# Moving ScalarE's part of weight conversions one step later, V's conversion one step sooner, and lam between the halves of q, in a kernel of linear attention and a mixer

## The chip, the cores and the metric

The kernel runs on one core of a Trainium2 chip. The metric is the device time of one execution in microseconds, the median of several. The kernel before took 690.38 us (689.95 to 690.59, 4 runs). The profile covers one execution and gives a span that is some 1.8 us shorter than the time. The granted clock is the share of its full clock that TensorE has by the profile; "half clock" means a stretch in which it is 0.5.

## The reference

Two blocks, one behind the other, shortened here to what they compute. The first is attention with a decay per head, in chunks of the sequence, the second a mixer: a low-rank product over the sequence, then two dense products with a ReLU between.

```python
# q, k, v: (4, 8, 768, 64); lam: (8,);  Dmask, lam_pow, rev_pow: powers of lam
out[chunk] = ((qb @ kb.T) * Dmask) @ vb + (qb * lam_pow) @ kv_state
kv_state   = lam_block * kv_state + (kb * rev_pow).T @ vb
x = out as (4, 768, 512)
h = x.transpose(0, 2, 1) @ U @ V          # U: 768x32, V: 32x768, float64 as w_ch1, w_ch2
u = x + h.transpose(0, 2, 1)
result = u + max(u @ w_ch1, 0) @ w_ch2    # 512 -> 2048 -> 512
```

The kernel works on 128 rows of the sequence at a time: 24 such steps, six for each of the four batches. U, V and the weights come as float64. The kernel reads them as pairs of 32-bit words and builds float32 from them by integer operations on VectorE and two ReLU passes on ScalarE that rebuild the exponent.

## The kernel before

What matters is the order of work within one step, because each engine runs its instructions in the order in which they were issued:

```python
pieces = [("prep", 0), ("scale", 0), ("scores", 0), ("inter", 0), ("masked", 0)]
for s in range(NS):
    ...
    step += [("prep", s + 1), ("scale", s + 1)] * more   # PE transposes pq, pk; ACT copies qt, kt; POOL qs, ks
    ...
    step += [("intra", s), ("state", s)]                 # PE px, pkv; ACT copy x_nat; DVE kv
    ...
    step += [("scores", s + 1)] * more                   # PE pss
    ...
    step += [("inter", s + 1), ("masked", s + 1), ("fade", s + 1)] * more   # PE px from kv; DVE sm; ACT faded
    step += [("aside", s)] * (done < 0)                  # conversion of U, V and the first weights
```

Each name stands for one product or operation of a step: pq and pk are the transposes of q and k, qt and kt their copies, pss the scores, sm the scores times the mask, px the output of the step (inter adds the part that comes from the state, intra the part from the step itself), pkv the step's addition to the state kv. qs and ks are q and k times their powers of lam, both made on GpSimd (POOL in the profile).

The conversion of one matrix is a list of pieces, each given a step in which it runs at the end, as "aside":

```python
def one():                                               # (cut)
    nc.vector.tensor_scalar(sc, hi, 20, 0x7FF, ALU.logical_shift_right, ALU.bitwise_and)
    nc.vector.tensor_scalar(m, hi, 0xFFFFF, 0x100000, ALU.bitwise_and, ALU.bitwise_or)
    nc.scalar.activation(out=sc_f, in_=sc, func=AF.Relu, bias=low_end, scale=-1.0)
    nc.scalar.activation(out=sc, in_=sc_f, func=AF.Relu, bias=high_end, scale=-float(1 << 23))
# two, three, four: one VectorE operation each; for V then
#   five:          vt = V's high bits (DVE), high(0): two ScalarE casts
#   low(1), low(3): two subtractions each on VectorE; high(2): two ScalarE casts
for steps, at in (
    (u_side, (0, 2, 2, 3, 3)),
    (v_steps(), (1, 2, 4, 4, 5, 5, 5, 6, 6, 6)),
    ...
```

Later, in step 6, `low(0)` forms pp (x times U), ScalarE copies it to pt, and `low_sum` forms pr from pt; in step 7, `mix(0)` forms pu from V and is the first to need all of V.

The start: lam is loaded behind the two halves of k on ScalarE's queue. One product (pl) spreads it over the partitions. VectorE then builds the mask (eight scans) and the powers powq (four scans) before the first masking. `keep_busy` runs products of a blank tile, four ahead of pl and one ahead of each half's transposes, so that TensorE isn't idle.

## Time and profile before

| | kernel before |
|---|---|
| time, median | 690.38 us |
| span of the profile | 688.6 us |
| TensorE busy | 674.0 us, 98% |
| TensorE idle, first 60 us | 10.3 us |
| waits of TensorE that the change aims at | lam 1.5, U's exponents 0.76, V's exponents 1.16, pt 1.91, V's low parts 2.52 us |
| stretches at half clock | one, 43.95 to 47.36 us |

TensorE is the bound, so only its idle time and its half-clock time can be won. The lines and their reading are in the prediction.

### The profile page before, as it was taken

Reading aid. Unit: us, or ns where it says so; the run is one execution under the profiler, and the core shown is the slowest. Engines: PE = TensorE matmul, PEld = TensorE weight load, DVE = VectorE, ACT = ScalarE, POOL = GpSimd, SP = SyncE. Lnnn points to the kernel's source line nnn. Section 1 sums busy time; section 2 is a strip of 40 time slices with the busy share of each in tenths; the row PEclk is TensorE's granted clock in tenths of the full one; section 3 lists DMA queues with packets and bytes.
Section 4 is the critical chain, followed back from the end, with each engine's and each line's share of the span. In section 5 each row is a group of like instructions: output and inputs, shape, how many; then the busy total and the mean of one; then the engine's idle time right before and its main releaser. Section 6 shows DMA issues by size and latency. Waiting matters only on the chain.

```text
span 688.6 us, 12580 instructions
## 1 busy us (share of the span) xinstructions
PE 674.0 (98%) x4818; PEld 546.5 (79%) x4818; DVE 498.8 (72%) x858; ACT 291.2 (42%) x543; POOL 112.2 (16%) x90
## 2 busy tenths in 40 slices
PE   7979999999999999999999999999999999999997
PEld 7858888877888888888888888888888888888885
DVE  5458888876999977777789355787586686866864
ACT  3556686645565644444456231232232322322320
POOL 3524676532000000000000000030030120300300
PEclk9999999999999999999999999999999999999999
DMA  9877887244576755556566999956354363453531
GB/s 213 198 166 187 212 212 189 69 137 171 183 273 232 272 201 198 207 205 207 205 233 241 317 299 381 327 173 186 96 184 131 92 208 99 137 169 96 165 92 61
DMA packets 131629, 131.24 MB, mean 191 GB/s; under 512 B 81330, under 2 KB 89522, under 8 KB 131570
## 3 DMA queue, kind: packets, MB, share of 16 engines
q1 hardware_dynamic: 130512, 130.18, 60.2%
q8 instruction: 38, 0.62, 0.4%
q10 hardware_dynamic: 1058, 0.26, 0.2%
q14 instruction: 21, 0.17, 0.1%
HBM read 80.09 MB, written 50.33 MB: 189 GB/s over the span
## 4 chain that ended last, share of the span: by engine, by line
PE 94%; DVE 3%; ACT 2%; issue 1%; DMA 0%; ACTq 0%; DVEq 0%
PE pz L676 26%; PE pz L809 13%; PE pz L807 13%; PE pd L686 13%; PE pd L811 13%; PE px L431 3%; PE pss L378 3%; PE put L494 2%; PE pkv L396 1%; PE px L419 1%; PE pq L338 1%; PE pk L338 1%; PE pu L477 1%; DVE sm L387 1%; PE pr L463 1%
## 5 line engine op out<-in xcount | busy, mean ns | idle before, releaser
L676 PE MATMUL pz<-u_hl,w 128*128 128x512 f32 x768 | 191.1, 398 | 0.2 <-ACT r L682 0.2
L676 PEld LDWEIGHTS pz<-u_hl,w 128*128 128x128 f32 x768 | 143.9, 188 | 36.2 <-ACT r L682 0.9
L809 PE MATMUL pz<-w_hl,m 128*128 128x512 f32 x384 | 151.6, 396 | 0.0
L807 PE MATMUL pz<-w_hl,m 128*128 128x512 f32 x384 | 151.6, 396 | 0.0
L811 PE MATMUL pd<-w_d,m 128*128 128x512 f32 x384 | 150.0, 396 | 0.0
L790 ACT ACTIVATE m<-mt 128x512 fp32r<-128x512 f32 x96 | 60.7, 632 | 195.6 <-PE pd L811 138.7
L791 DVE SCALAR_TENSOR_TENSOR m<-rm,m 128x512 fp32r<-128x512 f32 x96 | 71.5, 745 | 45.7 <-ACT m L790 45.4
L831 POOL TENSOR_TENSOR o<-o,u 128x512 f32<-128x512 f32 x20 | 29.8, 1522 | 447.5 <-DVE o L829 447.5
L691 DVE SCALAR_TENSOR_TENSOR r<-pd,r 128x512 f32<-128x512 f32 x96 | 61.8, 685 | 55.5 <-ACT r L682 41.2
L686 PE MATMUL pd<-u_d,w 128*128 128x512 f32 x384 | 98.2, 397 | 0.0
L807 PEld LDWEIGHTS pz<-w_hl,m 128*128 128x128 f32 x384 | 72.3, 188 | 17.7
L809 PEld LDWEIGHTS pz<-w_hl,m 128*128 128x128 f32 x384 | 72.3, 188 | 17.6
L811 PEld LDWEIGHTS pd<-w_d,m 128*128 128x128 f32 x384 | 72.3, 188 | 17.6
L686 PEld LDWEIGHTS pd<-u_d,w 128*128 128x128 f32 x384 | 72.2, 188 | 17.4
L682 ACT ACTIVATE r<-pz 128x512 f32<-128x512 f32 x96 | 52.0, 593 | 58.9 <-PE pz L676 58.9
L789 DVE TENSOR_SCALAR mt<-rm 128x512 uint32<-128x512 uint32 x96 | 46.2, 481 | 33.8 <-DMA rm<-r_d 33.6
L792 DVE SCALAR_TENSOR_TENSOR m<-m 128x512 fp32r<-128x512 f32 x96 | 69.0, 720 | 0.9
L192 ACT CAST w<-wt 128x512 fp32r<-128x512 f32 x32 | 19.9, 622 | 41.3 <-DVE wt L189 34.0
L387 DVE TENSOR_TENSOR sm<-pss,mask 128x512 f32<-128x512 f32 x48 | 30.7, 681 | 8.6 <-PE pss L378 8.6
L362 POOL TENSOR_TENSOR qs<-qt,powq 128x512 f32<-128x512 f32 x20 | 25.9, 1295 | 38.9 <-ACT qt L342 31.2
L431 PEld LDWEIGHTS px<-vraw,sm 128*64 128x64 f32 x768 | 25.2, 141 | 8.0 <-issue 4.1
L378 PE MATMUL pss<-qt,kt 64*128 64x128 f32 x384 | 28.6, 289 | 1.2 <-ACT kt L342 1.2
(87 smaller groups left out, 708.4 us busy)
## 6 DMA issues: line engine op xcount, KB each, us to landing
r_d<-r SPq DMA_DIRECT2D x96, 256.0 KB, 2.6
rm<-r_d SPq DMA_DIRECT2D x96, 256.0 KB, 2.7
words<-in_moe_w_ch_dram SPq DMA_DIRECT2D x30, 512.0 KB, 4.6
w_d<-w SPq DMA_DIRECT2D x16, 768.0 KB, 3.3
w_hl<-w_d SPq DMA_DIRECT2D x16, 512.0 KB, 6.5
vraw<-in_v_dram SPq DMA_DIRECT2D x24, 256.0 KB, 3.9
u_d<-x_nat SPq DMA_DIRECT2D x24, 256.0 KB, 3.3
u<-u_d SPq DMA_DIRECT2D x24, 256.0 KB, 4.2
```

What stands on the lines that cost most here:

```text
L378: nc.tensor.matmul(out=pss[:, x, a, :], lhsT=kt[half[x], a, :], rhs=qt[half[x], a, :], start=True, stop=True,)
L676: nc.tensor.matmul(out=acc[g][0], lhsT=w[:, n, ct, :], rhs=uhl[g][:, n, ct, :], start=(ct == 0 and n == 0), stop=(ct == CT - 1 and n == 1),)
L682: nc.scalar.mul(rs[g], acc[g][0], 1.0 + E)
L686: nc.tensor.matmul(out=acc[g][1], lhsT=w[:, 2, ct, :], rhs=ud[g][:, ct, :], start=(ct == 0), stop=(ct == CT - 1),)
L691: nc.vector.scalar_tensor_tensor(rs[g], acc[g][1], 4096.0, rs[g], ALU.mult, ALU.add)
L789: nc.vector.tensor_scalar(t.bitcast(U32), r.bitcast(U32), HI, None, ALU.bitwise_and)
L790: nc.scalar.activation(out=m[:, 0], in_=t, func=AF.Relu)
L791: nc.vector.scalar_tensor_tensor(m[:, 1], r, 0.0, hi, ALU.max, ALU.subtract)
L792: nc.vector.scalar_tensor_tensor(m[:, 2], hi, E, low, ALU.mult, ALU.subtract)
L807: nc.tensor.matmul(out=pz, lhsT=m[:, 0, cols], rhs=hl[:, 0], start=first, stop=False)
L809: nc.tensor.matmul(out=pz, lhsT=m[:, 1, cols], rhs=hl[:, 1], start=False, stop=end)
L811: nc.tensor.matmul(out=pd, lhsT=m[:, 2, cols], rhs=dd, start=first, stop=end)
```

## The change

The intent is to take ScalarE's conversion work out of the place where it stands between TensorE's transposes and their copies, to have V ready before the first mix (for which the last of V's low parts also moves from VectorE to GpSimd), and to start the chain from lam sooner. The diff, cut to its core:

```diff
+    late = []
+    def on_scalar(what):                      # now, or behind the next step's intra
+        if late and late[0] is None:
+            late.append(what)
+        else:
+            what()
 ...
-            nc.scalar.activation(out=sc_f, in_=sc, func=AF.Relu, bias=low_end, scale=-1.0)
-            nc.scalar.activation( ... )
+            def exponents():                  # the same two activations
+                ...
+            on_scalar(exponents)
 ...
+            if name == "q" and s == 0 and h == 0:
+                engine.dma_start(out=lam_row[:, 0:H], in_=lam.unsqueeze(0))
 ...
-        step += [("intra", s), ("state", s)]
+        step += [("intra", s), ("late", s), ("state", s)]
 ...
-            high(0)
+            on_scalar(lambda: high(0))
 ...
-            five, lambda: low(1), lambda: high(2), lambda: low(3)
+            five, lambda: low(1, nc.vector), lambda: on_scalar(lambda: high(2)),
+            lambda: low(3, nc.gpsimd),
 ...
-        (v_steps(), (1, 2, 4, 4, 5, 5, 5, 6, 6, 6)),
+        (v_steps(), (1, 1, 3, 3, 4, 4, 4, 5, 5, 5)),
 ...
+        late[:] = [None] * (s < NT)
         for step in side.pop(s, ()):
             step()
+        late[:] = late[1:]
 ...
-    nc.scalar.dma_start(out=lam_row[:, 0:H], in_=lam.unsqueeze(0))
 ...
-    keep_busy(4, "pq")
-    pl = one_bank([P, H], "pl", "pk")
+    keep_busy()                               # five blank products, none between the transposes any more
+    turn_half(0, 0, "q")                      # transposes of the first half of q, ahead of pl
+    pl = one_bank([P, H], "pl", "pt")
```

More of the change, by code (lines that the diff above doesn't have):

```diff
@@ L148, in one @@
             low_end, high_end = ends[-1][0:rows, 0:1], ends[-1][0:rows, 1:2]
-            nc.scalar.activation(out=sc_f, in_=sc, func=AF.Relu, bias=low_end, scale=-1.0)
-            nc.scalar.activation(
-                out=sc, in_=sc_f, func=AF.Relu, bias=high_end, scale=-float(1 << 23)
-            )
+            def exponents():
+                nc.scalar.activation(out=sc_f, in_=sc, func=AF.Relu, bias=low_end, scale=-1.0)
+                nc.scalar.activation(
+                    out=sc, in_=sc_f, func=AF.Relu, bias=high_end, scale=-float(1 << 23)
+                )
+            on_scalar(exponents)
         def two():
@@ L321, with keep_busy, turn_half @@
     half = [slice(0, D), slice(D, P)]
-    def keep_busy(n, tag="pss"):
-        out = (one_bank([P, C], "idle", tag) if tag == "pq" else two_banks("idle", tag)[:, 0])[:, 0:P]
-        for i in range(n):
-            nc.tensor.matmul(out=out, lhsT=blank, rhs=blank, start=True, stop=True)
-    def prep(s):
-        qt, kt = (att.tile([P, HP, P], FP32, tag=n, bufs=2, name=n) for n in ("qt", "kt"))
-        n = HP // parts(s)
-        for a0 in range(0, HP, n):
-            for name, dst, tag in (("q", qt, "pt" if a0 else "pq"), ("k", kt, "pu" if a0 else "pk")):
-                if s == 0:
-                    keep_busy(1)
-                pt = one_bank([P, n, P], "p" + name, tag)
-                for a in range(a0, a0 + n):
-                    nc.tensor.transpose(
-                        out=pt[:, a - a0, :], in_=raw[s, name][:, 2 * a : 2 * a + 2, :],
-                        identity=ident,
-                    )
-                nc.scalar.copy(dst[:, a0 : a0 + n, :], pt)
-        st[s].update(qt=qt, kt=kt)
+    def keep_busy():
+        out = one_bank([P, C], "idle", "pq")
+        for i in range(5):
+            nc.tensor.matmul(out=out[:, 0:P], lhsT=blank, rhs=blank, start=True, stop=True)
+    qts, kts = {}, {}
+    def turn_half(s, a0, name):
+        ts, tag = (qts, ("pq", "pt")) if name == "q" else (kts, ("pk", "pu"))
+        if a0 == 0:
+            ts[s] = att.tile([P, HP, P], FP32, tag=name + "t", bufs=2, name=name + "t")
+        n = HP // parts(s)
+        pt = one_bank([P, n, P], "p" + name, tag[a0 > 0])
+        for a in range(a0, a0 + n):
+            nc.tensor.transpose(
+                out=pt[:, a - a0, :], in_=raw[s, name][:, 2 * a : 2 * a + 2, :], identity=ident
+            )
+        nc.scalar.copy(ts[s][:, a0 : a0 + n, :], pt)
+    def prep(s):
+        for a0 in range(0, HP, HP // parts(s)):
+            for name in "qk":
+                if (s, a0, name) != (0, 0, "q"):
+                    turn_half(s, a0, name)
+        st[s].update(qt=qts.pop(s), kt=kts.pop(s))
         for name in "qk":
@@ L578, in high, with low @@
                 nc.scalar.copy(out, st["t"][rows])
-        def low(g):
+        def low(g, engine):
             for out, rows in parts((g,)):
-                nc.vector.tensor_tensor(
+                engine.tensor_tensor(
                     out=out, in0=st["v"][rows], in1=st["t"][rows], op=ALU.subtract
@@ L606, in aside, with on_scalar_late @@
     def aside(s):
+        late[:] = [None] * (s < NT)
         for step in side.pop(s, ()):
             step()
+        late[:] = late[1:]
+    def on_scalar_late(s):
+        for what in late:
+            what()
+        late.clear()
     ordered = ctx.enter_context(ExitStack())
@@ L630 @@
     powers()
-    run["aside"] = aside
+    run.update(aside=aside, late=on_scalar_late)
     for what, s in pieces:
```

## The prediction

> **What bounds the kernel now.** I read the page first, then the waits of TensorE, then the timeline around each of those waits, then busy time by stretches. From the page:
>
> ```profile
> PE 674.0 (98%) x4818; PEld 546.5 (79%) x4818; DVE 498.8 (72%) x858; ACT 291.2 (42%) x543; POOL 112.2 (16%) x90
> ...
> PE 94%; DVE 3%; ACT 2%; issue 1%; DMA 0%; ACTq 0%; DVEq 0%
> ```
>
> TensorE is the bound: 674.0 of 688.6 us busy, 94% of the chain that ended last. So a change that leaves its matmuls alone can win only TensorE's idle time (14.6 us), plus stretches in which it runs at half clock. The busy time by stretches (from 60 to 300 us: 239.7 of 240 us busy) puts most of the idle time into the first 60 us: 2.6 us in the first ten, then 0.9, 0.8, 1.2, 2.1 and 2.8. The waits of TensorE over the whole run name it:
>
> ```profile
> PE pu L477 <- DVE vp L582: 2.5, 1, 2.5
> PE pr L463 <- ACT pt L459: 1.9, 1, 1.9
> PE pl L626 <- DMA lam_row<-in_lam_dram: 1.5, 1, 1.5
> PE pkv L396 <- ACT kt L342: 1.2, 2, 0.8
> PE pss L378 <- ACT kt L342: 1.2, 1, 1.2
> ...
> PE px L431 <- DVE sm L387: 0.9, 2, 0.7
> ```
>
> (Who waited for whom: total us, times, longest.) Every wait the diff aims at is in this list. At the start, the timeline shows a chain:
>
> ```profile
> 1.85 0.61 ACTq L619 DMA_DIRECT2D lam_row<-in_lam_dram  x1
> ...
> 4.65 0.56 PE L626 MATMUL pl<-lam_row 1*128 1x8 f32 x2 [1.52 <-DMA lam_row<-in_lam_dram]
> ...
> 5.25 0.17 DVE L627 COPY lamb<-pl 128x8 f32<-128x8 f32 x1 [3.15 <-PE pl L626]
> 5.45 2.63 DVE L287 TENSOR_TENSOR_SCAN mask<-lamb,ident 128x128 f32<-128x128 f32 x8
> ...
> 8.37 2.22 POOL L351 TENSOR_TENSOR ks<-kraw,small 128x512 f32<-128x512 f32 x2 [7.06 <-DMA kraw<-in_k_dram]
> ...
> 8.58 2.93 DVE L300 TENSOR_TENSOR_SCAN powq<-small 128x128 f32<-128x128 f32 x4
> ...
> 11.43 1.26 DVE L387 TENSOR_TENSOR sm<-pss,mask 128x512 f32<-128x512 f32 x2
> ```
>
> lam is the third transfer on ScalarE's queue, behind both halves of k. Everything from the product with lam to the first masking is one VectorE chain without a gap; scores are ready at about 10.4 us, so VectorE sets the first px, not TensorE. The second kind of stall is ScalarE doing weight conversion between a transpose and its copy:
>
> ```profile
> 25.44 0.46 ACT L149 ACTIVATE sc<-sc,vp 128x192 f32<-128x192 uint32 x1 [0.99 <-DVE sc L145]
> ...
> 25.93 0.46 ACT L150 ACTIVATE sc<-sc,vp 128x192 uint32<-128x192 f32 x1
> ...
> 26.29 0.57 ACT L342 COPY qt<-pq 128x512 f32<-128x512 f32 x1
> 26.76 0.59 ACT L342 COPY kt<-pk 128x512 f32<-128x512 f32 x1
> ...
> 27.40 0.55 PEld L396 LDWEIGHTS pkv<-vraw,ks 128*64 128x64 f32 x16 [0.90 <-ACT kt L342]
> ```
>
> The copy qt was ready to start at about 25.2; it waits for VectorE's sc and for two exponent passes. The same happens with V's exponents at 35.09 to 36.26, and with V's high copy (the two L578 casts, 41.32 to 42.35) ahead of the copy pt, which holds pr to 42.88. Then, twice the damage of that wait:
>
> ```profile
> 40.54:43.95 3.41, 1.50 (x8) 0.50 (x6) 0.71 (x2) 2.45 (x5) 0.56 (x1) 0.99 0.82 195
> 43.95:47.36 3.41, 3.41 (x55) 3.29 (x56) 1.81 (x3) 1.29 (x3) 1.15 (x2) 0.51 0.02 3
> 47.36:50.78 3.42, 2.43 (x54) 2.01 (x52) 2.53 (x5) 3.08 (x8) 1.28 (x2) 1.00 0.51 127
> ```
>
> (Busy us of PE, PEld, DVE, ACT, POOL, then the granted clock.) After a stretch with 1.50 us of TensorE work the clock is 0.51 for 3.41 us.
>
> **What the Trainium skill says.** (1) "TensorE: Matmul & The Clock Gate", Part 1, has a clock gate that drops to half after an idle window of about 3.4 us, a free-running one, and starts in that state. The trace agrees: half clock for 3.41 us above, and the first transposes are 421 ns each against 272 later, until about 9.6 us. (2) The same page, "Architectural detail", calls ScalarE and VectorE strict FIFO. The trace agrees: qt sits behind the exponents although its transpose had ended. (3) "SBUF — State Buffer", "Who interferes with whom": a VectorE operation with two SBUF inputs, or in a two-port mode, and a GpSimd operation that reads SBUF exclude each other. The trace agrees: the powq scans take 392 to 1209 ns, the longest while ks runs, and at 54.78 us a conversion takes 1.03 us beside ks where its twin takes 0.42. (4) "DMA: Bandwidth & Descriptors", "Queues, rings and completion order": SP and ACT each own one ring on the same 16 engines, descriptors consumed in ring order. So lam behind one half of q should land sooner than behind two of k; the trace of before shows only the second: 1.85 to about 4.5 us.
>
> **The change, part by part.**
>
> *Start.* lam moves behind the first q half on SP's queue: issue at about 1.3 instead of 1.85, landing at my estimate 3.6 instead of 4.5 (q halves take a median 2.9 us to landing from 0.74). TensorE first does five blank products instead of four (8 passes took 2.08 us, so 10 take about 2.5: 1.05 to 3.55), then two transposes at 0.21 spacing, then pl, 0.56: end about 4.6 instead of 5.21. The VectorE chain moves as a block, sm and px with it: 0.6 us. The four single blank products (8 passes at 0.21 = 1.7 us) leave prep, which only gives TensorE slack ahead of sm: worth nothing on the path.
>
> *U's exponents* go behind the next step's x_nat copy. There ScalarE has about 4.29 us per step and 2.84 us of work (0.59 x 3 + 1.07), so 0.92 us fits. Removes the 0.76 us wait of pkv.
>
> *V's exponents* (2 x 0.61) likewise, in step 4: 2.84 + 1.22 = 4.06, just inside 4.29. Removes 1.16 us.
>
> *V's first high copy* (1.03 us) runs in step 5, before pp exists. Then pt can follow pp at once: the 40.97 to 42.88 gap goes, 1.91 us. With it goes the reason for the half clock. What that cost, from the same groups elsewhere on the chain: px 1.90 against 1.08, pkv 0.85 against 0.47, pss 1.40 against 1.09, pr 1.13 against 0.86: 0.82 + 0.38 + 0.31 + 0.27 = 1.78 us.
>
> *V's low parts* move a step earlier, and two of the four go to GpSimd. Now they take 49.51 to 52.74 on VectorE and hold mix until 52.30. With them in step 5 and the second high copy (1.05 us) after x_nat of step 6, mix finds all ready: pkv, pss, px and transposes (0.47 + 1.09 + 0.62 + 1.03 = 3.2 us) lie between intra and mix, the copies need 0.59 + 1.05. Removes 2.52 us.
>
> Sum of gains: 0.6 + 0.76 + 1.16 + 1.91 + 1.78 + 2.52 = 8.7 us. After 60 us TensorE is busy throughout, so what is won there should reach the end whole.
>
> *New costs, estimates.* Step 3 now carries on VectorE both U's last two operations and V's first three: 0.35 + 0.36 + 0.34 + 0.35 + 0.55 = 1.95 us, in a gap between sm and the next kv add of some 1.98 us, with GpSimd's qs (1.28) and ks falling into it. I take 0.7 us of new wait there. And at the start TensorE loses the blank products and will have done scores and the next transposes by about 8.5 us, then idle until px at about 11.5: 3 us, near the stretch that cost the clock at 40.54. Half clock for one such stretch costs 1.7 us; at a little under one chance in two, 0.8 us. 8.7 - 0.7 - 0.8 = 7.2.
>
> **Rivals.** (a) *All 8.7 us arrive*: 681.8. For it: the waits are single and named, and ScalarE and GpSimd have room. Against: VectorE's step 3 is full to the brim. (b) *The cold start and VectorE eat half*: the clock is slow from 11 to 15 us and kv waits behind V's conversion for one GpSimd operation after another: minus 1.7 and minus 2.0, so 685.5. For it: the scans beside ks took two to three times as long. Against: the freed TensorE work gives prep room, and the released clock may come earlier than 9.6 us. (c) *Transfers become the bound in the first 40 us*, where the DMA share is 0.9 to 1.0 and q, k and v alone are 768 KB per 4.29 us: gains vanish until 40 us, leaving 6.2 - 0.7: 685. Against: q for step 7 is issued at 25.95 and used at 39.88, nine microseconds after landing, and no TensorE wait there names a DMA but lam's. (d) *Nothing*, the waits merely moving: 690. Against: the engine after each wait is TensorE itself, with 100% busy stretches behind.
>
> **Range and chances.** Middle between (a) and (b), nearer (a): 683.3 us, 1.0% less. The range 681.3 to 686.3 runs from all gains plus a little more clock to both costs and half a microsecond. Over 2% needs under 676.7, more than all idle time of the first 60 us: 1%. Slower by 2%: 1%, only if the order creates a stall I don't see.
>
> **What would show it.** Right: no wait of pr on pt, of pu on vp or of pss on kt among TensorE's waits; granted clock 1.00 between 35 and 50 us; lamb starting at about 4.65, sm at about 10.8; step 0 to the first mix shorter by some 7 us. Wrong: px of step 0 at half clock; kv in step 3 behind V's conversion with TensorE waiting over a microsecond; pq or pk waiting for a DMA; the first lam product still after 5 us.

## The result, and the profile after

The changed kernel took 686.70 us (686.65 to 686.76, 4 runs) against 690.38 us: 3.7 us or 0.5% less, by the ratio 0.9948 (95% interval 0.9930 to 0.9965). A ratio here is the mean time of one kernel's runs over that of the other's in the same rounds, so it is not quite the ratio of the medians. The prediction was 683.3 us with a range of 681.3 to 686.3; the time lies just outside.

The page of the changed kernel, its busy time and the engines of the chain that ended last:

```profile
PE 675.0 (99%) x4812; PEld 547.1 (80%) x4812; DVE 499.4 (73%) x856; ACT 291.5 (43%) x543; POOL 114.1 (17%) x92
...
PE 96%; DVE 2%; ACT 1%; issue 1%; DVEq 0%
```

TensorE is busy 1.0 us longer than before although it has six instructions fewer: some of its work ran slower. Its waits over the whole run (total us, times, longest):

```profile
PE px L439 <- DVE kv L424: 2.1, 1, 2.1
PE px L451 <- DVE sm L407: 1.9, 2, 1.6
PE idle L341 <- DVE blank L642: 1.1, 1, 1.1
PE pkv L416 <- ACT kt L356: 0.4, 1, 0.4
```

Every wait that the change aimed at is gone: no pu on vp, no pr on pt, no pss on kt, no pl on lam. One is new, px on kv, 2.1 us, and the wait of the first px for sm has grown from 0.9 to 1.9. The timeline around the new wait (start, duration, engine, operation; the last bracket is the idle time before it):

```profile
31.33 1.28 POOL L382 TENSOR_TENSOR qs<-qt,powq 128x512 f32<-128x512 f32 x1 [3.02 <-DMA kraw<-in_k_dram]
31.39 1.43 DVE L153 TENSOR_SCALAR sc<-words 64x384 uint32<-64x384 uint32 x1
...
32.56 2.30 POOL L371 TENSOR_TENSOR ks<-kraw,small 128x512 f32<-128x512 f32 x2
32.74 1.21 DVE L154 TENSOR_SCALAR m<-words 64x384 uint32<-64x384 uint32 x1
...
33.98 1.29 DVE L170 SCALAR_TENSOR_TENSOR m<-words,m 64x384 f32<-64x384 uint32 x1
...
35.20 0.41 DVE L424 TENSOR_TENSOR kv<-pkv,faded 128x256 f32<-128x256 f32 x1
...
35.76 0.69 PE L439 MATMUL px<-kv,qs 64*64 64x64 f32 x32 [2.10 <-DVE kv L424]
```

The same three operations of V in the kernel before:

```profile
34.72 0.34 DVE L145 TENSOR_SCALAR sc<-words 64x384 uint32<-64x384 uint32 x1
34.98 0.35 DVE L146 TENSOR_SCALAR m<-words 64x384 uint32<-64x384 uint32 x1
...
35.36 0.55 DVE L158 SCALAR_TENSOR_TENSOR m<-words,m 64x384 f32<-64x384 uint32 x1
```

V's first three operations, 0.34, 0.35 and 0.55 us long in the kernel before, take 1.43, 1.21 and 1.29 us. Each of them ends just after a GpSimd operation ends: the first after qs (32.61), the second after the first ks (some 33.7), the third after the second ks (34.86). kv is issued behind them and can't pass.

Busy time in stretches (PE, PEld, DVE, ACT, POOL, then the granted clock and two figures of the transfers) shows what follows from waits:

```profile
9.85:13.27 3.42, 1.52 (x37) 1.15 (x36) 2.49 (x5) 0.86 (x2) 1.66 (x2) 1.00 0.99 225
13.27:16.68 3.41, 3.41 (x54) 3.07 (x54) 0.72 (x2) 1.65 (x5) 1.06 (x1) 0.50 1.01 230
33.70:37.10 3.40, 1.34 (x39) 1.30 (x40) 3.37 (x6) 0.42 (x1) 1.17 (x2) 1.00 0.78 178
37.10:40.52 3.42, 3.42 (x44) 2.98 (x44) 1.07 (x3) 2.06 (x4) 1.98 (x2) 0.51 0.94 225
```

There are now two stretches at half clock, each behind one in which TensorE had 1.3 to 1.5 us of work. The one of before, at 43.95, is gone. And the start:

```profile
1.24 0.39 SPq L272 DMA_DIRECT2D lam_row<-in_lam_dram  x1
...
4.27 0.59 PE L654 MATMUL pl<-lam_row 1*128 1x8 f32 x2
...
4.90 0.17 DVE L655 COPY lamb<-pl 128x8 f32<-128x8 f32 x1 [2.81 <-PE pl L654]
...
11.08 1.25 DVE L407 TENSOR_TENSOR sm<-pss,mask 128x512 f32<-128x512 f32 x2
```

lam isn't waited for any more (it has landed by 4.27 us; before, pl waited for it until 4.65), and the whole VectorE chain is 0.35 us sooner (sm at 11.08 against 11.43).

The start times of the same instructions in both traces show where the difference arises:

| TensorE reaches | before, us | after, us | after minus before | what lies between |
|---|---|---|---|---|
| first px | 12.14 | 11.79 | -0.35 | lam sooner |
| pq, issued in step 1 | 15.88 | 17.05 | +1.17 | half clock from 13.27, +1.5 |
| pq, issued in step 4 | 29.73 | 29.92 | +0.19 | U's exponents out of the way, -1.0 |
| pq, issued in step 5 | 34.02 | 36.38 | +2.36 | kv wait, +2.2 |
| pq, issued in step 6 | 39.88 | 42.51 | +2.63 | V's exponents -1.3, half clock from 37.10 +1.6 |
| pr | 42.88 | 43.44 | +0.56 | pt no longer waited for, -2.1 |
| pq, issued in step 7 | 48.70 | 47.66 | -1.04 | half clock of before gone, -1.6 |
| first pu (mix) | 52.30 | 48.51 | -3.79 | V's low parts ready, -2.75 |

The two sizes that share a row are told apart by the second half-clock stretch itself: pk to px took 0.73 us instead of 0.44, px to pss 1.90 instead of 1.08, pss to pp 1.58 instead of 1.09, together 1.6 us. After the first mix nothing of size is added or lost; the end differs by 3.7 us.

### The profile page after: what moved, and what is told of

It reads as the page before. It is cut to its first block, busy times and chain, and to the rows that moved or that the text cites. A ratio compares the mean times of both kernels' runs of the same rounds, so it can differ in the third digit from the quotient of the medians.

```text
span 684.9 us, 12572 instructions
## 1 busy us (share of the span) xinstructions
PE 675.0 (99%) x4812; PEld 547.1 (80%) x4812; DVE 499.4 (73%) x856; ACT 291.5 (43%) x543; POOL 114.1 (17%) x92
## 4 chain that ended last, share of the span: by engine, by line
PE 96%; DVE 2%; ACT 1%; issue 1%; DVEq 0%
PE pz L704 26%; PE pz L837 13%; PE pz L835 13%; PE pd L714 13%; PE pd L839 13%; PE px L451 3%; PE pss L398 3%; PE put L514 2%; PE px L439 2%; PE pq L353 1%; PE pkv L416 1%; PE pk L353 1%; PE pu L497 1%; PE pp L465 1%; PE pr L483 1%
## 5 line engine op out<-in xcount | busy, mean ns | idle before, releaser
L451 PE MATMUL px<-vraw,sm 128*64 128x64 f32 x768 | 28.7, 229 | 1.9 <-DVE sm L407 1.9
```

The lines of the kernel that those rows point to most:

```text
L451: nc.tensor.matmul(out=px[half[t], x, a, :], lhsT=sm[:, x, a, half[t]], rhs=vr[:, 2 * a + x, :], start=(first and a == 0), stop=(a == HP - 1),
```

## The experiments

Theory: the change removes all the waits it aims at (some 9 us, with the half clock behind one of them), and gives back about 5 us in three places: a half-clock stretch at the start, made by TensorE's longer idle time there; the kv wait, made by GpSimd shutting VectorE out of one operation after another; and a second half-clock stretch, made by that wait. Rivals: the clock falls for reasons other than idle time; VectorE simply has too much to do in step 3; the parts that bring V sooner are needed, so that every mending costs them again.

Twelve runs were made, four at a time. Each group shared its runs of the kernel before, 7 of them, medians 691.15 (e1 to e4), 689.83 (e5 to e8) and 689.91 us (e9 to e12). All results were correct. Each diff is against the changed kernel, unless said otherwise. The kernel before differs by up to 1.3 us between the groups, and e11 shows the changed kernel to differ as much from run to run, so gains of a microsecond or less against its first 686.70 us are not told apart from that.

**e1_fill_start**

```diff
+        step += [("fill", 6)] * (s == 0)      # six blank products
         step += [("intra", s), ("late", s), ("state", s)]
```

> The changed kernel with six blank products (12 passes, about 1.3 us warm) put between the transposes of step 1 and the first px, where TensorE waits 1.64 us for VectorE's masking. Theory (the idle stretch 9.85 to 13.27 us held only 1.53 us of TensorE work, so the clock fell to half from 13.27 to 16.66 us): px still starts at 11.8 us, pkv, scores and inter of step 0 run at full clock, 1.5 us gained, 685.2 us. If the earlier kv wait then also falls otherwise into the 3.41 us stretches, up to 3.1 us gained, 683.6. Rival (the half clock comes from something else than idle time, or the fillers delay px): 686.7 or more.

Measured: 685.15 us (685.13 to 685.20), ratio 0.9924. The stretches of this run (columns as above):

```profile
9.85:13.27 3.42, 2.14 (x43) 1.81 (x43) 2.47 (x5) 0.23 (x1) 1.64 (x2) 1.00 0.97 220
13.27:16.68 3.41, 3.41 (x82) 2.99 (x78) 1.71 (x3) 2.06 (x6) 1.06 (x1) 1.00 1.09 245
```

px still starts at 11.77 us; pkv, pss and inter of step 0 now run at full clock. The kv wait (2.11 us) and half clock behind it stayed. The expected 1.5 us came, by filling idle time with useless work. The time alone doesn't show it: without any filling two of the four runs of e11 take 685.21 and 685.49 us. What shows it is a comparison with e4, which has no filling here and whose stretches of 3.41 us lie within 0.1 us of those of e1. The stretch with the wait in e1, then the one with it and the next in e4:

```profile
8.44:11.85 3.41, 2.39 (x22) 2.20 (x23) 3.41 (x6) 1.07 (x2) 2.35 (x3) 1.00 1.00 226
8.54:11.96 3.42, 1.07 (x11) 0.84 (x11) 3.42 (x6) 1.07 (x2) 2.37 (x3) 1.00 1.11 251
11.96:15.37 3.41, 3.24 (x51) 2.94 (x52) 0.69 (x2) 0.59 (x1) 0.83 (x2) 0.50 1.00 228
```

**e4_fill_kv_wait**

```diff
         step += [("scores", s + 1)] * more
+        step += [("fill", 8)] * (s == 4)
```

> The changed kernel with eight blank products (about 1.8 us) put before the inter of step 5, where TensorE waits 2.10 us for kv. Theory (the second half clock, 37.1 to 40.5 us, follows from the idle time of that wait): the wait for kv itself stays, px starts at 35.8 as before, the clock stays 1.00, about 1.6 us gained: 685.1 us. Rival (the clock falls for another reason): 686.7.

Measured: 685.00 us (684.89 to 685.17), ratio 0.9922. px behind kv starts at 35.59 us, the granted clock is 1.00 from 33.7 to 43.9. So the second half-clock stretch comes from the kv wait, and costs 1.7 us on top of the wait's own 2.1. In all six profiles with the kv wait unfilled (the first, e1, e6, e7, e10, e11) a stretch at half clock follows it.

**e3_ks_after_v**

```diff
-        if s + 1 < NS:
+        if s + 1 in (NT, NT + 1):
+            st[s + 1] = {}
+        elif s + 1 < NS:
             scale_k(s + 1)
 ...
+        if s == NT - 1:                       # in aside, behind V's low parts
+            scale_k(NT)
+            scale_k(NT + 1)
```

> The changed kernel with GpSimd's ks of steps 6 and 7 held back until after V's low parts, so that in step 3 only qs meets V's conversion on VectorE. Theory (mutual exclusion: sc waits for qs, m for the first ks, the last for the second ks): sc stays long, the two behind it take 0.35 and 0.55 us, the kv wait falls from 2.10 to about 0.55 us, and with it the half clock at 37.1 goes: 683.5 us, 684.5 if the clock still falls. Rival (VectorE simply has too much work in that gap, 1.95 us in 1.98): the wait stays at about 2 us, 686.7.

Measured: 683.93 us (682.41 to 684.50), ratio 0.9903. VectorE's operations behind sc in the timeline of this run:

```profile
31.21 0.34 DVE L154 TENSOR_SCALAR m<-words 64x384 uint32<-64x384 uint32 x1
31.58 0.55 DVE L170 SCALAR_TENSOR_TENSOR m<-words,m 64x384 f32<-64x384 uint32 x1
32.06 0.41 DVE L426 TENSOR_TENSOR kv<-pkv,faded 128x256 f32<-128x256 f32 x1
```

With no ks beside them the second and third operation are back at 0.34 and 0.55 us, while sc, which still meets qs, takes 1.42. The wait before px falls from 2.10 to 0.50 us. VectorE has the same work as in the changed kernel, so it isn't the amount of work: it is the GpSimd operations beside it. No half clock follows. The runs lie 2 us apart; see e11.

**e2_v_one_step_later**

```diff
-        (v_steps(), (1, 1, 3, 3, 4, 4, 4, 5, 5, 5)),
+        (v_steps(), (1, 1, 4, 4, 5, 5, 5, 5, 5, 5)),
```

> The changed kernel with V's conversion begun in step 4 rather than 3 (steps 1,1,4,4,5,5,5,5,5,5), ScalarE's parts still late, the last low parts still on GpSimd. Theory (kv of step 4 waits 2.10 us behind V's three operations on VectorE, each shut out by one GpSimd operation; the half clock at 37.1 us follows from that wait): no wait of px on kv, granted clock 1.00 from 17 us on, 2.1 + 1.6 us gained; a new wait of mix of up to 1 us is possible because the low parts end later: 683.0 to 684.0 us. Rival (moving V sooner was needed, the wait for the low parts comes back): mix waits about 2 us and the time stays at 685 to 687.

Measured: 684.87 us (683.42 to 685.06), ratio 0.9915: a gain of 1.8 us, half of the 3.7 that the theory had. The kv wait of step 4 and the half clock behind it are gone, and mix doesn't wait. But GpSimd's low parts, 2.57 us long and now at the time of step 6, hold qs, and px waits 0.9 us for it; ScalarE's four casts in a row hold the copies, and pkv waits 1.0 us for kt in two places instead of 0.4. The expectation had looked for the new wait at mix only.

**e7_old_start**

The changed kernel with the start of before: lam third on ScalarE's queue, blank products between the transposes.

> The changed kernel with the start of before (lam third on ScalarE's queue, four single blank products among the transposes); everything later as changed. Theory (the new start is worth 0.35 us and costs a stretch of half clock, 1.5 us, because the blank products were what kept TensorE's time filled until px): px starts at 12.1, full clock from 13.3 to 16.7, kv wait 2.1 us as in the changed kernel: 685.5 us. Rival (the new start is a gain): 687.0 or more.

Measured: 685.53 us (684.62 to 685.70), ratio 0.9933. The first px starts at 12.30 us instead of 11.79, but pkv, pss and inter behind it run at full clock, and the time is 1.2 us less than the first 686.70. Against e11 it is 0.35 us less, with runs that overlap, and e11's two runs of the same mean clock (685.21 and 685.49 us at 0.997) are as fast as e7's (685.45 to 685.70 at 0.997 and 0.998). So the new start wins nothing as it stands; that it is a loss is not shown.

**e8_late_only**

The kernel before with nothing but ScalarE's parts put late:

```diff
-        step += [("intra", s), ("state", s)]
+        step += [("intra", s), ("late", s), ("state", s)]
 ...
+            on_scalar(exponents)              # and on_scalar for high(0), high(2)
```

> The kernel before with one part of the change: ScalarE's parts of U's and V's conversion put behind the next step's x_nat copy; start, V's steps and engines as before. Theory: the waits of pkv (0.76), pss (1.16) and pr (1.9) go, and with the last the half clock after it (1.8), in sum 5.6 us; mix still waits 2.5 us for V's low parts; no kv wait in step 5: 684.8 us, less than the whole change takes. Rival (late without sooner delays V, mix waits longer and eats it): 687 or more.

Measured: 683.62 us (683.53 to 683.71), ratio 0.9908. One part of the change alone takes 6 us off, more than the whole. The waits of pss and pr are gone, none of px on kv is there, and V's low parts still hold mix, for less time than before:

```profile
PE pu L488 <- DVE vp L593: 1.5, 1, 1.5
```

So beside late, bringing V sooner can win at most these 1.5 us at mix, and it pays 2.1 + 1.6 us for them at the kv wait and behind it.

**e6_powers_after_mask**

```diff
-    pieces = [("prep", 0), ("scale", 0), ("scores", 0), ("inter", 0), ("masked", 0)]
+    pieces = [("prep", 0), ("scale", 0), ("scores", 0), ("inter", 0), ("masked", 0), ("powers", 0)]
 ...
-    powers()
```

> The changed kernel with one reordering: powers() (four scans, 2.93 us beside ks) behind the first masking on VectorE. Theory (the start is bound by VectorE's chain, not by lam's arrival, and of that chain the first px doesn't need powq): sm starts at about 8.2 us, px at about 10.1, TensorE doesn't idle and the stretch from 13.3 us runs at full clock: 1.7 + 1.5 us gained, 683.5 us; the kv wait of 2.1 us stays, the half clock behind it may come or go with where the stretches fall. Rival (qs, which needs powq, takes its place): inter of step 1 waits for GpSimd over 2 us, and the time stays at 686 or more.

Measured: 682.77 us (681.84 to 683.42), ratio 0.9895, 3.9 us less than the changed kernel. The first masking starts at 8.37 us, px at 9.54; inter of step 1 waits 0.84 us for qs and starts at 13.14 instead of 16.27. There is a gain on the side: behind the masking the four scans no longer meet ks, and take 1.37 us together instead of 2.93. The kv wait stays, 2.11 us, with a half-clock stretch in this profile.

**e5_all_mended**

The changed kernel with e6's and e3's edits, V at (1, 1, 3, 4, 4, 4, 4, 5, 5, 5), and `late` for s < NT + 2.

> The version that the first four runs point to: the changed kernel with powers() put behind the first masking on VectorE, GpSimd's ks of steps 6 and 7 held back until after V's low parts, V's third operation a step later (1,1,3,4,4,4,4,5,5,5), and ScalarE's part put late in steps 6 and 7 too. Theory: px of step 0 starts at about 10.1 instead of 11.8 us and no stretch runs at half clock (1.7 + 1.5 us), no kv wait and no half clock after it (2.1 + 1.6), the last kt wait (0.4) gone: 686.7 - 7.3 = 679.4 us, at most 681. Rival (each mended wait only uncovers the next, as the change itself did): 682 to 684.

Measured: 684.22 us (682.22 to 685.00), ratio 0.9908: missed by nearly 5 us. Up to 42 us everything went as expected (the first mix at 41.58 us, 6.9 us sooner than in the changed kernel, no kv wait, full clock). Then the rival came true: the first operation on w1's words waited 3.6 us on VectorE for a transfer that SP had issued only at 44.41 us, sm stood behind it, px waited 2.6 us, and half clock followed. The faster front had run into the transfers.

**e9_words_later**

e5 with one more edit:

```diff
-        (w1_steps(0, True), (3, 4, 5, 6, 7, 8, 9, 10, 12, 13, 14)),
+        (w1_steps(0, True), (3, 4, 5, 6, 8, 9, 10, 11, 12, 13, 14)),
 ...
-        late[:] = [None] * (s < NT + 2)
+        late[:] = [None] * (s < NT + 3)
```

> e5 with the first operation on w1's words a step later (step 8 instead of 7), ScalarE's part late up to step 8. In e5 that operation sat on VectorE until 47.7 us for a transfer that SP had issued at 44.4, sm waited behind it, px 2.6 us, and half clock followed. Theory: that was e5's only new bound; without it the runs with full clock lie at 682.2 - 2.6 = 679.6 us, and no wait over 1 us is left but the first: 679.4 to 680.5. Rival (transfers bind the whole front once the stalls are gone): pq, pk or px wait for q, k or v somewhere between 40 and 60 us, 681.5 to 683.

Measured: 680.13 us (680.11 to 680.39), ratio 0.9858. This is the best version: 1.4% faster than the kernel before, against 0.5% for the change. Two of its four TensorE waits (the others are 1.1 us at the very start and 0.2 us); the first is inter of step 1 at 13.15 us, as in e6 (the view names faded, in e6 qs; the two end within 0.02 us of each other, and the product reads qs):

```profile
PE px L441 <- ACT faded L393: 0.8, 1, 0.8
PE px L453 <- DVE sm L409: 0.3, 1, 0.3
```

**e12_late_and_start**

The changed kernel with e6's edit, and with V's steps and engines as before: (1, 2, 4, 4, 5, 5, 5, 6, 6, 6), low(3) on VectorE.

> ScalarE's parts late and the new start with powers() behind the first masking, but V's steps and engines as before: e8's and e6's halves together. Theory: no kv wait, mix waits about 1.5 us for V's low parts as in e8, inter of step 1 comes 2.1 us sooner than in e8: 683.6 - 2.1 = 681.5 us. Rival (with the faster start the low parts or the words for U come late): 683 or more.

Measured: 681.72 us (681.67 to 681.89), ratio 0.9880. As expected: pu waits 1.5 us, nothing waits for kv, and all four runs lie within 0.2 us. Without bringing V sooner one comes within 1.6 us of the best version.

**e10_low_on_vector**

```diff
-            lambda: low(3, nc.gpsimd),
+            lambda: low(3, nc.vector),
```

> The changed kernel with V's last low part on VectorE again instead of GpSimd. Theory (this part of the change is off the path either way, since mix now comes 4 us after the low parts): the same within 0.3 us, 686.7, with 2.1 us of kv wait. Rival (GpSimd's part was what let mix start in time): mix waits about 1 us for vp, 687.5 or more.

Measured: 687.69 us (686.24 to 687.83), ratio 0.9961. Neither side was quite right. Mix doesn't wait for vp, as the theory had it, but the low parts (one of them 1.53 us long) keep VectorE from the next kv, and px waits 0.7 us for that. Three of the four runs show a mean clock of 0.994 or 0.995, two half-clock stretches as in the changed kernel. Compared with e11, of the same group, the move to GpSimd is worth 1.8 us by the medians; 0.7 us of it is this wait, and the rest is not separated here from the clock.

**e11_changed_again**

The changed kernel, unaltered.

> The changed kernel once more, on this chip, to compare its clock from run to run: the experiments fall into groups 0.85 to 1.7 us apart, as the mean granted clock reads 1.000, 0.997 or 0.995. If the stretches of 3.41 us are not tied to the program's start, some runs lie below 686.7, at 685 to 686; if they are tied, all four lie within 0.2 us of it.

Measured: 685.88 us; the four runs are 685.21, 685.49 (mean clock 0.997), 686.27 and 686.61 us (0.995), ratio 0.9940. In its profile pkv, pss and inter of step 0 run at full clock, although TensorE waited 1.55 + 0.26 us there as in the first profile. So what a given idle time costs varies from run to run. The traces show what varies. Within a profile the clock changes only at points that are whole multiples of 3.41 us apart (13.25, 16.66, 37.14 and 40.55 in the first profile), and where this grid lies differs between profiles. Counted back from its own half clock at 34.40, e11's grid cuts the start at 10.50 and 13.92, and the stretch between holds 1.89 us of TensorE work. In e2 it cuts at 10.25 and 13.66, and the stretch holds 1.60. First e11, then e2:

```profile
10.50:13.92 3.42, 1.89 (x50) 1.68 (x52) 1.82 (x6) 0.81 (x2) 1.26 (x1) 1.00 0.94 214
13.92:17.33 3.41, 3.41 (x82) 3.06 (x84) 1.71 (x3) 2.25 (x7) 1.45 (x2) 1.00 1.06 240
...
10.25:13.66 3.41, 1.60 (x46) 1.47 (x48) 2.09 (x5) 0.77 (x2) 1.27 (x1) 1.00 1.09 246
13.66:17.07 3.41, 3.41 (x58) 2.95 (x54) 1.44 (x3) 1.46 (x5) 1.06 (x1) 0.50 1.12 252
```

The longest wait of the kernel before, 2.52 us for V's low parts, falls across two stretches of the grid and is followed by full clock:

```profile
47.32:50.73 3.41, 2.47 (x54) 2.05 (x52) 2.48 (x5) 3.12 (x8) 1.27 (x2) 1.00 0.51 125
50.73:54.15 3.42, 1.84 (x49) 1.63 (x49) 2.67 (x3) 0.24 (x1) 1.01 (x1) 1.00 0.65 148
54.15:57.56 3.41, 3.41 (x67) 3.02 (x63) 3.12 (x6) 2.02 (x5) 1.06 (x1) 1.00 0.56 158
```

In the profiles that show a half-clock stretch, from 8.4 to 60 us, every full-clock stretch of the grid with at most 1.60 us of TensorE work is followed by half clock, and none with 1.84 us or more; none lies between. The kernel before varies in the same way: in the second group it took 688.78 us at 1.000, 689.7 to 689.9 at 0.997 and 691.51 at 0.994. One half-clock stretch is 3.41 us at half speed, that is 3.41 x 0.5 / 688 = 0.0025 of the mean clock, and 1.7 us of TensorE's time, less where it waits anyway.

## Why the prediction was wrong, and where it was right

**What bounds the kernel** was right: TensorE's idle time and half-clock time in the first 60 us are the whole matter, and what was won by the first mix (3.79 us) arrived at the end (3.7).

**The gains** were right in kind and nearly in size. Predicted 8.7 us in six terms; by the table of start times: start 0.35 (predicted 0.6), U's exponents 1.0 (0.76), V's exponents 1.3 (1.16), pt 2.1 (1.91), half clock at 44 us 1.6 (1.78), V's low parts 2.75 (2.52). That is 9.1 us. The start was the one term too large: pl ended at 4.86 us rather than 4.6, because the transposes ahead of it began at 3.69 and pl itself only at 4.27.

**The new costs** were the step that failed. The prediction put them at 0.7 + 0.8 us. They measured 5.3.

- "I take 0.7 us of new wait there", in step 3: the wait was 2.1 us (2.2 in the table). The mechanism was named, VectorE's gap "full to the brim" with qs and ks falling into it, and rival (b) even had its size, 2.0. But 0.7 us is less than what a single collision added (1.43 instead of 0.34 us), and in fact three VectorE operations met three GpSimd operations in turn, and each took 1.2 to 1.4 us. e3 shows it: with two of the three taken away, two operations are at their old length and 1.6 us of the wait go.
- "at a little under one chance in two, 0.8 us", for the clock at the start: all four first runs of the changed kernel have a mean clock of 0.995, two stretches, and this one cost 1.5 us. That it came in all four was partly chance: in e11 two runs of four have it by their mean clock. e1 shows that new blank products take it away, and the kernel before, whose grid lies within 0.1 us of the first profile's, that the old ones do (2.48 us of work between 9.77 and 13.19, full clock, against 1.52 and half); e7 doesn't show it, since on its grid (10.99 to 14.40) the start of e11, without such products, holds 2.37 us and would keep full clock too. That the single blank products are "worth nothing on the path" was wrong: not the path, but the clock needed them.
- Missing altogether: the half clock behind the kv wait, 1.6 us. The prediction had read the very same thing in the kernel before (pr's wait of 1.9 us, then 3.41 us at half clock) and had booked its removal as a gain, but didn't apply it to the wait that it was itself adding. e4 shows the two are separable: fill the wait, and 1.7 us come back with the wait in place.

The sum of the measured terms is 9.1 - 2.2 - 1.5 - 1.6 = 3.8 us; measured, 3.7.

**Rivals.** (b) was nearest: "The cold start and VectorE eat half". One of the prediction's own signs of being wrong came true: kv behind V's conversion, "with TensorE waiting over a microsecond". (c), transfers as the bound, was not the answer for this change, but it is what stopped e5 once the other waits were gone. (d), waits merely moving, is half true: two fifths of the gain stayed.

**The range** was too narrow by 0.4 us above for the first four runs. Three of the four runs of e11 fall below its upper end: a range for one kernel should have held the 1 to 2 us by which the clock alone moves the time. (A slip in its sums: 2% less than 690.38 is 676.6, not 676.7.)

**A part against the whole.** The prediction took the five parts of the change as things that add up. They don't: late alone gives 683.6 (e8), late with V sooner and the new start 686.7 (685.9 in e11). With GpSimd's ks out of VectorE's way, powq out of the first masking's way and the words later, all parts together reach 680.1. What lam's earlier load is worth alone is not shown: no run had the old start with powq behind the first masking, and e6's 3.9 us can be powq's place alone.

What stays open: how much of e10's 1.8 us is due to its own wait, where between 1.60 and 1.84 us of work the clock's border lies, and what places the grid (it differs between the profiles of one kernel).

## What to carry to other kernels

When work is moved in time, look up what the other engines do at its new place, and where VectorE operations meet GpSimd's, count each at the length of the one it meets, not at its own (here 1.43 us instead of 0.34). Book a long wait of TensorE with the half-clock stretch that may follow it (here 1.6 to 1.7 us; whether it follows depends on how the wait falls on the grid), for waits that a change adds as well as for those it removes; blank products in an idle gap are worth keeping until the gap itself is gone. Of a change with several parts, try each alone: here one part was worth more than the whole.

## What the Trainium skill lacked or had wrong

- "TensorE: Matmul & The Clock Gate", Part 1: the free-running stretch of some 3.4 us at half clock agrees (3.41 us; its place differs between runs, e11). Its closing table tells to avoid idle gaps of over about 3 us; here gaps of 1.91 us (before), 1.64 + 0.26 us (after) and 2.10 us (after) were followed by a whole stretch at half clock, and one of 2.52 us (before), split between two stretches, wasn't. The page speaks of an idle stretch; what it lacks is how much work one may hold: here those with up to 1.60 us in 3.41 were followed by half clock, those with 1.84 or more not.
- "SBUF — State Buffer", "Who interferes with whom": that one of the two engines, VectorE or GpSimd, blocks the other for the whole instruction agrees. The page has this for VectorE operations with two SBUF inputs, such as the third here, and for those in a two-port mode; whether the first two, which read one input, are in such a mode is not shown. What it lacks is what a row of operations on both sides does: one VectorE operation got through for each GpSimd operation, so 0.34, 0.35 and 0.55 us became 1.43, 1.21 and 1.29 us.
